# Chunks 0 and 1 as a pair: all eight units in the prologue, and chunk 1's second layer in a stretch of its own

## The chip, the cores and the metric

One NeuronCore of one Trainium2 chip runs the kernel. The metric is the device time of one execution in microseconds (us), lower is better. Engines are named as in the profile: PE (TensorE, the matmul array), PEld (its weight loads), DVE (VectorE), ACT (ScalarE), POOL (GpSimd), SP (the engine that here only issues DMAs); "ACTq" and "SPq" are the DMA-issuing sides of ACT and SP.

## The reference

Decayed linear attention over blocks of 64 tokens, and behind it a two-layer feed-forward network with softplus. 4 batches, 8 heads, 768 tokens, 64 dims a head; the network is 512 to 2048 to 512 over 3072 tokens. All of it is float32.

```python
for b in range(nb):                                   # blocks of 64 tokens, in order
    intra = (qb @ kb.T * Dmask) @ vb                  # Dmask[i,j] = lam**(i-j), lower triangle
    inter = (qb * lam_pow) @ kv_state
    out[:, :, sl] = intra + inter
    kv_state = lam**64 * kv_state + (kb * rev_pow).T @ vb
...
h = x @ w_in                                          # x: (3072, 512) from out
g = np.maximum(h, 0) + np.log1p(np.exp(-np.abs(h)))   # softplus
return g @ w_out
```

## The kernel before, in words

**Tiling.** The 768 tokens are six chunks of 128 tokens (two blocks of each of the 4 batches, so 512 rows for the network). The 8 heads are four pairs. A *unit* g is one chunk of one head pair: g = 4·chunk + pair, 24 units, each of two 512-KB loads (`load_upto`). A unit runs `q_decay` and `k_decay`, the scores and state products on PE (`mm_scores`, tiles x and y), `mask_scores`, the state update (`update_states`, which needs the state of the unit four earlier), then `mm_out` (tile z), which gives the network's input for that head pair. An `event(g)` is the output set of unit g−1 and the scores and update of unit g.

**The products of the network** are made of float32 values split in a high and a low part: three matmuls for each product. A weight matrix is 16 blocks f; block (f, 0) is of the first layer (A f in the change's lists) and (f, 1) of the second (B f). Each comes from DRAM as 64-bit words of 512 KB (`w_load`) and is converted on chip: `w_scale` and `w_round` on ACT, `w_shift`, `w_sign` and `w_add` on DVE, `w_hi` on ACT, `w_lo` on DVE; in the loop always for a pair of blocks at once, in the order of `w_order`.

**The chunks.** Chunks 0 and 1 use the plain network: `mlp1` is a first-layer block (12 matmuls of 128x512), `chain_act`, `chain_hi`, `chain_lo` make its softplus and the two parts, `mlp2` is the second-layer block (12 matmuls into four accumulators). Chunks 2 and 3, and 4 and 5, go as pairs whose first layer is done with seven products of half-size blocks (P1 to P7, L629), and the last pair's second layer too (L1014). These need sums of weight blocks (`block_sums`/`store_sums`/`send_sums`, or the same work as `box_sums`/`box_parts`/`box_send`), which are made on DVE and ACT during the earlier chunks, sent to DRAM (g1, g2 for the first layer, v for the second), and loaded back (`load_w1`); the converted blocks themselves go the same way (`store_blocks` to g1, g2, g3; `load_w2` brings second-layer blocks back).

**What sets the order.** Each engine works through its own instructions in the order in which the program writes them, and waits by semaphores. There is no planner: the prologue is a list of steps written out (L480 to L492, names resolved by the table at L472), the rest is loops. Before: the prologue has units 0 to 4 and first-layer blocks 0 to 3 of chunk 0. Then a loop over s = 4 to 31 (s // 16 is the chunk, s % 16 the block): the chain of block s−1, a conversion of the next weight pair, the second-layer block s−4, a unit now and then, and the first-layer block s; chunk 0 goes first, chunk 1 behind it. The sums for first-layer blocks 0 to 5 are made in chunk 1's part of that loop. In the first chunk the carry of the state from its first block to its second is made on PE: a matmul with zeros opens the accumulator (L306), and two matmuls with a diagonal matrix add the decayed state (L359); ACT copies the result (L364).

Of the kernel before, what the change touches and what calls it, by code (L numbers as in the profile page):

```python
# [7 lines left out]
F32 = mybir.dt.float32  # L8
# [7 lines left out]
C = 128  # L16
# [7 lines left out]
LAG = 4  # L24
STD = 2
# [7 lines left out]
def decay_attention_softplus_ffn(  # L33
# [119 lines left out]
    keep_warm(18)  # L153
# [22 lines left out]
    def powers(out, n):  # L176
# [125 lines left out]
    def mm_scores(g, x, y):  # L302
        q, k, kd, v = q_of(g), k_of(g), kds.pop(g), vt_of(g)
        if first_chunk(g):

            nc.tensor.matmul(y[lo], lhsT=warm[hi, :64], rhs=warm[hi], start=True, stop=False)  # L306
        for b in range(B):
            for t in range(2):
                cols = slice((2 * b + t) * 64, (2 * b + t + 1) * 64)
                for s in range(2):  # L310
                    r = half(s)
                    nc.tensor.matmul(x[r, cols], lhsT=k[r, b, t], rhs=q[r, b, t], start=True, stop=True)  # L312
                    if s == 0 or not last_chunk(g):
                        nc.tensor.matmul(
                            y[half(1 - s), cols], lhsT=kd[r, b, t], rhs=v[r, b, t],
                            start=s == 0 or not first_chunk(g), stop=s == 0 or not first_chunk(g),
                        )
# [37 lines left out]
    def carry_states(g, y):  # L355
        st = states[g]
        u = y[lo].rearrange("q (b t e) -> q b t e", b=B, t=2)
        for t in range(2):
            nc.tensor.matmul(  # L359
                u[:, :, t], lhsT=diag[hi, heads(g).start + t], rhs=st[hi, :, t], start=False, stop=t == 1  # L360
            )
# [37 lines left out]
    h_tiles, l_tiles, g_tiles, o_tiles = {}, {}, {}, {}  # L399

    def chain_act(s):
        l_tiles[s] = tl([128, 512], F32, f"l{s}")
        nc.scalar.activation(l_tiles[s], h_tiles.pop(s), AF.Softplus)  # L403

    def chain_hi(s):
        g_tiles[s] = t4([128, 2, 512], F32R, f"g{s}")
        nc.scalar.copy(out=g_tiles[s][:, 0, :], in_=l_tiles[s])  # L407

    def chain_lo(s):
        g = g_tiles[s]  # L410
        nc.vector.tensor_sub(out=g[:, 1, :], in0=l_tiles.pop(s), in1=g[:, 0, :])  # L411

    def mlp1(s, ps_=range(NP)):
        c, f = divmod(s, NF)
        if s not in h_tiles:
            h_tiles[s] = bank(f"h{s}")
        w = w_of(f, 0)
        for p in ps_:
            cs = slice(p * 128, (p + 1) * 128)
            x = x_of(c, p)  # L420
            for n, (i, j) in enumerate(((0, 0), (1, 0), (0, 1))):
                nc.tensor.matmul(  # L422
                    h_tiles[s], lhsT=w[:, i, cs], rhs=x[:, j, :],
                    start=p == 0 and n == 0, stop=p == NP - 1 and n == 2,
                )
# [661 lines left out]
```

## Time and profile before

Three runs took 584.24 to 584.87 us, median 584.67. The profiled execution took 585.31, of which the trace spans 583.4 from the first instruction to the last; its granted TensorE clock is 1.000.

| engine | busy us | share of the span | instructions |
|---|---|---|---|
| PE | 567.5 | 97% | 5155 |
| DVE | 394.3 | 68% | 612 |
| ACT | 277.7 | 48% | 446 |
| POOL | 4.1 | 1% | 11 |

The DMA queues moved 148.64 MB. In rows of the trace a name left of the arrow is what is written, right of it what is read; L and a number is the line of the kernel. Rows of groups end with the busy time, the mean of one instruction in ns, and the idle time of the engine just before them with what ended it. Matmuls overlap in the array, so the mean of one is longer than the distance from one start to the next.

### The profile page before, as it was taken

The numbers are of one execution on the slowest core, as the hardware profiler recorded it, in microseconds if no ns is written. First come the engines' busy times: TensorE is split into PE (matmuls) and PEld (weight loads), VectorE is DVE, ScalarE is ACT, GpSimd is POOL, SyncE is SP. The second block draws the span as 40 slices with busy tenths as digits, with TensorE's granted clock in tenths as the row PEclk, the third lists the DMA queues.
The fourth block names the chain that finished last, engine by engine and source line by source line (L and its number), as shares of the span: only waits on it lengthen the run. The fifth ranks groups of instructions, "written<-read, shape, count | busy, mean of one in ns | idle before, by whom it ended". The sixth has DMA issues, their size and how long they took to land.

```text
span 583.4 us, 12175 instructions
## 1 busy us (share of the span) xinstructions
PE 567.5 (97%) x5155; PEld 460.1 (79%) x5155; DVE 394.3 (68%) x612; ACT 277.7 (48%) x446; POOL 4.1 (1%) x11
## 2 busy tenths in 40 slices
PE   8999989999999999999999999999999999999997
PEld 6677767788888887887878888866888888788886
DVE  7779998975667867476655765459623646748983
ACT  3777776663445445444344433436323333454441
POOL 2000000000000000000000000000000000000000
PEclk9999999999999999999999999999999999999999
DMA  8997555899999678477774878699797336911701
GB/s 292 406 408 289 183 203 175 271 326 341 334 396 406 238 248 308 142 269 285 249 255 163 300 242 285 245 302 317 298 398 281 129 122 217 383 53 51 274 37 72
DMA packets 52534, 148.64 MB, mean 255 GB/s; under 512 B 4480, under 2 KB 20864, under 8 KB 46464
## 3 DMA queue, kind: packets, MB, share of 16 engines
q1 hardware_dynamic: 40384, 133.19, 63.1%
q10 hardware_dynamic: 12096, 14.68, 7.4%
q8 instruction: 40, 0.66, 0.4%
q14 instruction: 14, 0.11, 0.1%
HBM read 110.10 MB, written 37.75 MB: 253 GB/s over the span
## 4 chain that ended last, share of the span: by engine, by line
PE 74%; DVE 10%; DMA 9%; ACT 2%; ACTq 2%; issue 1%; SPq 1%; DVEq 0%
PE rP L1014 13%; PE o L648 13%; PE b L629 11%; PE h L422 10%; PE o L443 9%; PE c L629 7%; PE a L629 7%; DMA raw<-in_wts 5%; DMA g<-w 2%; PE x L312 2%; PE z L327 2%; DMA att<-in_att 2%; ACTq L573 2%; PE z L331 1%; DVE c L236 1%
## 5 line engine op out<-in xcount | busy, mean ns | idle before, releaser
L648 PE MATMUL o<-w,g 128*128 128x512 f32 x432 | 105.8, 394 | 2.0 <-DVE g L640 1.2
L422 PE MATMUL h<-x,w 128*128 128x512 f32 x384 | 94.7, 396 | 3.0 <-DVE w L243 2.1
L648 PEld LDWEIGHTS o<-w,g 128*128 128x128 f32 x432 | 79.9, 188 | 21.8 <-DVE g L640 3.3
L422 PEld LDWEIGHTS h<-x,w 128*128 128x128 f32 x384 | 70.9, 188 | 20.8 <-DVE w L243 3.7
L443 PE MATMUL o<-w,g 128*128 128x512 f32 x336 | 82.0, 393 | 1.1 <-DVE w L243 0.8
L1014 PE MATMUL rP<-sP,vP 128*128 128x512 f32 x336 | 76.3, 389 | 0.0
L443 PEld LDWEIGHTS o<-w,g 128*128 128x128 f32 x336 | 62.5, 188 | 15.0 <-DVE w L243 1.1
L1014 PEld LDWEIGHTS rP<-sP,vP 128*128 128x128 f32 x336 | 63.1, 188 | 13.1
L629 PE MATMUL b<-xcP,w1b 128*128 128x512 f32 x192 | 49.1, 391 | 1.3 <-DVE act L951 0.8
L629 PE MATMUL a<-xcP,w1a 128*128 128x512 f32 x192 | 48.8, 389 | 0.0
L403 ACT ACTIVATE l<-h 128x512 f32<-128x512 f32 x32 | 19.1, 598 | 58.9 <-PE h L422 56.3
L629 PEld LDWEIGHTS b<-xcP,w1b 128*128 128x128 f32 x192 | 35.8, 188 | 9.9 <-DVE ta L802 1.4
L629 PEld LDWEIGHTS a<-xcP,w1a 128*128 128x128 f32 x192 | 36.1, 188 | 7.5
L411 DVE TENSOR_TENSOR g<-l,g 128x512 fp32r<-128x512 f32 x32 | 22.0, 689 | 24.6 <-ACT g L407 24.5
L339 DVE TENSOR_TENSOR a<-x,mask 128x512 f32<-128x512 f32 x15 | 10.4, 691 | 38.6 <-PE x L312 20.3
L951 DVE TENSOR_TENSOR act<-b,ta 128x512 f32<-128x512 f32 x8 | 5.5, 691 | 31.1 <-PE b L629 31.1
L894 ACT CAST sP<-act 128x512 fp32r<-128x512 f32 x32 | 19.2, 619 | 13.0 <-PE rP L1014 6.8
L640 DVE TENSOR_TENSOR sP<-act,sP 128x512 fp32r<-128x512 f32 x32 | 20.9, 686 | 6.6 <-ACT sP L894 6.6
L629 PE MATMUL c<-xcP,w1b 128*128 128x512 f32 x96 | 24.4, 390 | 0.0
L629 PE MATMUL b<-xcP,w1a 128*128 128x512 f32 x96 | 24.4, 389 | 0.0
L629 PE MATMUL c<-xcP,w1a 128*128 128x512 f32 x96 | 24.4, 389 | 0.0
L387 ACT COPY xr<-z 128x512 f32<-128x512 f32 x16 | 9.4, 585 | 30.4 <-PE z L331 30.0
(133 smaller groups left out, 881.5 us busy)
## 6 DMA issues: line engine op xcount, KB each, us to landing
att<-in_att SPq DMA_DIRECT2D x48, 512.0 KB, 6.8
w<-g SPq DMA_DIRECT2D x23, 1024.0 KB, 7.9
raw<-in_wts SPq DMA_DIRECT2D x32, 512.0 KB, 10.2
w1a<-g SPq DMA_DIRECT2D x16, 1024.0 KB, 6.6
g<-w SPq DMA_DIRECT2D x24, 512.0 KB, 8.4
w1b<-g SPq DMA_DIRECT2D x16, 768.0 KB, 7.0
vP<-box ACTq DMA_DIRECT2D x32, 256.0 KB, 4.3
vP<-vP SPq DMA_DIRECT2D x8, 1024.0 KB, 8.4
```

The lines of the kernel that those rows point to most:

```text
L312: nc.tensor.matmul(x[r, cols], lhsT=k[r, b, t], rhs=q[r, b, t], start=True, stop=True)
L327: nc.tensor.matmul(w[half(t), s, cols], lhsT=st[r, b, t], rhs=qd[r, b, t], start=True, stop=False)
L403: nc.scalar.activation(l_tiles[s], h_tiles.pop(s), AF.Softplus)
L411: nc.vector.tensor_sub(out=g[:, 1, :], in0=l_tiles.pop(s), in1=g[:, 0, :])
L422: nc.tensor.matmul(h_tiles[s], lhsT=w[:, i, cs], rhs=x[:, j, :], start=p == 0 and n == 0, stop=p == NP - 1 and n == 2,)
L443: nc.tensor.matmul(o_tiles[c][b], lhsT=g[:, i, b * 128 : (b + 1) * 128], rhs=w[:, j], start=f == 0 and n == 0, stop=f == NF - 1 and n == 2,)
L573: nc.scalar.dma_start(out=v_sums[p][:, i], in_=parts[:, :, n])
L629: nc.tensor.matmul(to, lhsT=w[:, k, n, p * 128 : (p + 1) * 128], rhs=x[:, j, p], start=start and p == 0 and m == 0, stop=p == 1 and m == 2 ...
L640: nc.vector.tensor_sub(out=g[:, 1], in0=l, in1=g[:, 0])
L648: nc.tensor.matmul(outs[c, b], lhsT=g[:, i, b * 128 : (b + 1) * 128], rhs=w[:, j], start=f == 0 and n == 0, stop=f == NF - 1 and n == 2,)
L894: nc.scalar.copy(out=g[:, 0], in_=of)
L1014: nc.tensor.matmul(to, lhsT=w[:, k, x, n * 128 : n * 128 + 128], rhs=g[:, y], start=fresh and i == 0 and m == 0, stop=i == NF // 2 - 1 and ...
```

## The change

Chunks 0 and 1 are worked as a pair, and the state carry of the first chunk moves from PE to DVE.

- `w_order` begins with A0 to A3 and then takes two second-layer blocks B and two first-layer blocks A in turn. The first loads are A0, unit 0, A1, units 1 to 4, A2 and A3, units 5 and 6; the rest are issued inside the lists.
- The zero matmul, the diagonal matrix and its matmuls go; `carry_states`, `update_first` and `update_second` are pairs of DVE instructions.
- The prologue's list (not quoted whole: 16 lines of such steps as `m 1 2`, block 1 of chunk 0 with head pair 2) now holds all eight units of chunks 0 and 1, the first-layer blocks 0 to 6 of both chunks (`m`, `n`), second-layer blocks 0 to 3 of chunk 0 (`l2`), and the sums of box 0. The first warm-up has 24 matmuls in place of 18; further ones in the list are 8 in place of 13.
- The loop runs f = 7 to 15. Each turn has first-layer block f of chunk 0 and of chunk 1, a second-layer block of chunk 0 three or more blocks behind, a weight pair, and box sums. Chunk 1's softplus results wait in SBUF (`late_act`). Unit 8's scores and events 9 to 11 stand at f = 9, 11, 13, 15.
- Chunk 1's second layer follows in one stretch, with events 12 to 16 at f = 1, 4, 7, 10, 13, and with the inputs of chunks 2 and 3's products.
- All eight second-layer boxes are made in the loop of chunks 2 and 3; before, two of them were made in chunk 3's second-layer stretch, and boxes (0, 6) and (0, 7) in that loop. First-layer boxes are sent by ACT's queue (`box_send`); before, six of eight went by SP's.

The core of the diff:

```diff
-    w_order = [(f, 0) for f in range(LAG)]
-    for f in range(2):
-        w_order += [(f, 1), (f + LAG, 0)]
-    for f in range(2, NF, 2):
-        w_order += [(f, 1), (f + 1, 1)]
-        if f + LAG < NF:
-            w_order += [(f + LAG, 0), (f + LAG + 1, 0)]
+    w_order = [(f, 0) for f in range(4)]
+    for f in range(4, NF, 2):
+        w_order += [(f - 4, 1), (f - 3, 1), (f, 0), (f + 1, 0)]
+    w_order += [(f, 1) for f in range(NF - 4, NF)]
...
-    for n in range(NP - 1):
-        load_upto(n + 1)
-        w_load(n + 1)
-    load_upto(NP)
-    w_load(7)
-    load_upto(NP + 1)
+    w_load(1)
+    load_upto(1)
+    w_load(2)
+    load_upto(5)
+    w_load(4)
+    load_upto(7)
...
-        if first_chunk(g):
-
-            nc.tensor.matmul(y[lo], lhsT=warm[hi, :64], rhs=warm[hi], start=True, stop=False)
...
     def carry_states(g, y):
-        for t in range(2):
-            nc.tensor.matmul(
-                u[:, :, t], lhsT=diag[hi, heads(g).start + t], rhs=st[hi, :, t], start=False, stop=t == 1
-            )
-    def next_states(g, y):
-        nc.scalar.copy(out=states[g][lo].rearrange("q b t d -> q (b t d)"), in_=y[lo])
+        decayed(g, states[g][lo], states[g][hi], hi, y[lo].rearrange("q (b t e) -> q b t e", b=B, t=2))
+    def update_first(g, y):
+        decayed(g, states[g][hi], states[g][lo], lo, y[hi].rearrange("q (b t e) -> q b t e", b=B, t=2))
+    def update_second(g, y):
+        states[g + NP] = th([128, B, 2, D], F32, f"st_{g + NP}")
+        decayed(g, states[g + NP][lo], states[g][hi], hi, y[lo].rearrange("q (b t e) -> q b t e", b=B, t=2))
...
+    def late_act(f):
+        if f // 4 not in late_l:
+            late_l[f // 4] = t8([128, 4, 512], F32, f"lb1_{f // 4}")
+        nc.scalar.activation(late_l[f // 4][:, f % 4], h_tiles.pop((1, f))[0], AF.Softplus)
...
-    for s in range(LAG, last):
...
+    conv_at = {7: [(12, 13), (14, 15)], **{f: [(2 * f, 2 * f + 1)] for f in range(8, NF)}}
+    box_of = {8: 1, 9: 2, 10: 3, 11: 4, 12: 5, 14: 6}
+    event_of = {9: 2 * NP, 11: 2 * NP + 1, 13: 2 * NP + 2, 15: 2 * NP + 3}
+    n_l2 = 4
+    for f in range(7, NF):
+        unit = event_of.get(f)
+        if unit is not None:
+            k_decay(unit)
+            q_decay(unit)
+        for ks in converting:
+            w_hi(*ks)
+            w_lo(*ks)
+        mlp1(0, f)
+        converting = conv_at[f]
+        for ks in converting:
+            w_scale(*ks)
+            w_round(*ks)
+            w_shift(*ks)
+            w_sign(*ks)
+        chain_act(f)
+        chain_hi(f)
+        for ks in converting:
+            w_add(*ks)
+        chain_lo(f)
+        mlp1(1, f)
+        if boxed and f >= 8:
+            box_parts((0, boxed[0]))
+        if f in box_of:
+            box_sums((0, box_of[f]))
+        if n_l2 < f - 3:
+            second0(n_l2)
+            n_l2 += 1
+        late_act(f)
+        if unit is not None:
+            if unit == 2 * NP:
+                scores_of(unit)
+                keep_values(unit)
+            else:
+                event(unit)
+                second0(n_l2)
+                n_l2 += 1
+        if boxed and f >= 8:
+            box_send((0, boxed.pop(0)))
...
+    box_sums((0, 7))
+    store_second(7)
+    load_w2(0)
+    load_w2(1)
+    second0(NF - 3)
+    second0(NF - 2, NF - 1, ends=True)
+    box_parts((0, 7))
+    events = {3 * n + 1: 3 * NP + n for n in range(NP + 1)}
...
+    for f in range(NF - 2):
...
+        if f in extra:
+            extra[f]()
+        run(seconds(1, [(f, gs.pop(f), w2_tiles[f // 2][:, f % 2])]))
+        if f in events:
+            event(events[f])
...
-        box_at = [(0, NF // 2 - 2), (0, NF // 2 - 1)] + [(1, i) for i in range(2, NF // 2)]
+        box_at = [(1, i) for i in range(NF // 2)]
...
-            if f in (2, 4):
-                box_sums((1, f // 2 - 1))
```

Three places in the order of instructions. First ACT, from the end of turn f = 7 to f = 8 of the new loop, after the change. Names: l and g are chunk 0's softplus result and its high part, lb the late results of chunk 1, w the weight casts of `w_hi` (w_1204 is B4 and B5, w_1207 is A8 and A9), c and raw the conversion of the next pair.

```order
L384 ACTIVATE l_1175<-h_7_1152 128x512
L388 CAST g_1177<-l_1175 128x512
L398 ACTIVATE lb_1_995<-h_7_1182 128x512
L222 CAST w_1204<-c_1165 128x1024
L222 CAST w_1207<-c_1170 128x1024
L201 ACTIVATE c_1223<-raw_1196 128x1024
```

The same place on PE, after the change (h_7_1152 is chunk 0's block 7, h_7_1182 chunk 1's; o are the accumulators of the second layer):

```order
L409 MATMUL h_7_1182<-x_0_646,w_1001 128x512 x6
L409 MATMUL h_7_1182<-x_1_839,w_1001 128x512 x6
L409 MATMUL h_8_1210<-x_0_306,w_1207 128x512 x6
L409 MATMUL h_8_1210<-x_1_461,w_1207 128x512 x6
L409 MATMUL h_8_1234<-x_0_646,w_1207 128x512 x6
```

Block 8 of chunk 0 stands directly behind block 7 of chunk 1, whose softplus (lb_1_995) stands on ACT ahead of the casts of block 8's weights. Before the change each turn of the loop had one first-layer and one second-layer block, and ACT had no late results.

Second, DVE from the box sums of turn f = 9 to the conversion of f = 10, after the change (a is unit 8's masked scores, st its states, w_1400 the low part of A10 and A11):

```order
L513 TENSOR_TENSOR box_2_1326<-w_942 128x512 x2
L516 TENSOR_TENSOR box_2_1326<-box_2_1326 128x256
...
L319 TENSOR_TENSOR a_1379<-w_1346,mask 128x512
L324 SCALAR_TENSOR_TENSOR st_717<-st_717,lam_c,w_1346 64x4x64 x2
L324 SCALAR_TENSOR_TENSOR st_1383<-st_717,lam_c,w_1346 64x4x64 x2
L226 TENSOR_TENSOR w_1400<-c_1300,w_1400 128x1024
L209 TENSOR_SCALAR c_1416<-c_1416 128x1024
```

The low part of the weights of the next first-layer block stands behind the box sums and unit 8's mask and states.

Third, PE where chunk 1 ends and chunks 2 and 3 begin (a, b and c are the accumulators of the seven-product layer, xc its inputs). Before the change, behind the scores of event 16:

```order
L422 MATMUL h_2813<-x_0_758,w_1342 128x512 x6
L422 MATMUL h_2813<-x_1_1180,w_1342 128x512 x6
L648 MATMUL o_0_1808<-w_6_2532,g_2548 128x512 x3
...
L648 MATMUL o_3_1811<-w_6_2532,g_2677 128x512 x3
L629 MATMUL a_0_2880<-xcP_2170,w1a_2709 128x512 x6
L629 MATMUL b_0_2881<-xcP_2703,w1a_2709 128x512 x6
```

After the change, behind the same scores:

```order
L292 MATMUL x_2784<-att_2587 64x64
L294 MATMUL y_2785<-att_2587,kd_2710 64x64
L621 MATMUL a_0_2859<-xcP_2267,w1a_2590 128x512 x6
L621 MATMUL b_0_2860<-xcP_2692,w1a_2590 128x512 x6
L621 MATMUL c_0_2875<-xcP_2434,w1a_2590 128x512 x6
```

A first-layer block and two second-layer blocks of chunk 1 stood between the last scores and the first product; now nothing does.

More of the change, by code (lines that the diff above doesn't have):

```diff
@@ L452, in w_group, with second @@
-    def w_group(j):
-        return (2 * j, 2 * j + 1) if 2 * j < NW else ()
-    def scores_of(g):
-        w = work(f"w{g}")
-        mm_scores(g, w[:, 0], w[:, 1])
-        mask_scores(g, w[:, 0])
-        update_states(g, w[:, 1])
+                    to, lhsT=w[:, i, cs], rhs=x[:, j, :],
+                    start=not done and n == 0, stop=len(done) == NP - 1 and n == 2,
+                )
+            done.append(p)
+    n_second = {}
+    def second(c, f, b, g, w):
+        if (c, b) not in outs:
+            outs[c, b] = obank(f"o{c}_{b}")
+        k = n_second[c, b] = n_second.get((c, b), 0) + 1
+        for n, (i, j) in enumerate(((0, 0), (0, 1), (1, 0))):
+            nc.tensor.matmul(
+                outs[c, b], lhsT=g[:, i, b * 128 : (b + 1) * 128], rhs=w[:, j],
+                start=k == 1 and n == 0, stop=k == NF and n == 2,
+            )
@@ new lines, in finish, with seconds @@
+    def finish(c, b):
+        if c not in obs:
+            obs[c] = t8([128, B, 512], F32, f"ob{c}")
+        nc.scalar.copy(out=obs[c][:, b], in_=outs[c, b])
+        nc.scalar.dma_start(out=out[b * S + c * C : b * S + (c + 1) * C, :], in_=obs[c][:, b])
+    def seconds(c, fs, ends=False):
+        work_ = []
+        for f, g, w in fs if not ends else ():
+            work_ += [lambda f=f, g=g, w=w, b=b: second(c, f, b, g, w) for b in range(B)]
+        if ends:
+            for b in range(B):
+                for f, g, w in fs:
+                    work_.append(lambda f=f, g=g, w=w, b=b: second(c, f, b, g, w))
+                work_.append(lambda b=b: finish(c, b))
+        return work_
@@ L462, in decay_attention_softplus_ffn, with run, second0 @@
+    def run(work_, n=None):
+        for _ in range(len(work_) if n is None else min(n, len(work_))):
+            work_.pop(0)()
+    def second0(*fs, ends=False):
+        run(seconds(0, [(f, g_tiles.pop(f), w_of(f, 1)) for f in fs], ends))
     xy, z = {}, {}
@@ L576, in box_send @@
             nc.scalar.dma_start(out=g2[i][:, :, 1:3], in_=parts[:, :, 2:4])
-    def send_sums(i):
-        parts = ready.pop(i)
-        nc.sync.dma_start(out=g1[i][:, :, 2:4], in_=parts[:, :, 0:2])
-        nc.sync.dma_start(out=g2[i][:, :, 1:3], in_=parts[:, :, 2:4])
-    w1_tiles, w2_tiles = {}, {}
+    w1_tiles = {}
+    steps_of = {
+        "q": q_decay, "k": k_decay, "xy": begin, "a": lambda p: mask_scores(p, xy[p][0]),
+        "st": lambda p: first_states(p, xy[p][1]), "z": end, "dl": lambda p: carry_states(p, xy[p][1]),
+        "uh": lambda p: update_first(p, xy[p][1]), "ul": lambda p: update_second(p, xy[p][1]),
+        "xh": lambda p: x_high(p, z[p]), "xl": lambda p: x_low(p, z[p]),
+        "scale": w_scale, "round": w_round, "shift": w_shift, "sign": w_sign, "add": w_add, "hi": w_hi, "lo": w_lo,
+        "act": chain_act, "ghi": chain_hi, "glo": chain_lo, "bct": late_act, "l2": second0,
+        "m": lambda f, p: mlp1(0, f, (p,)), "n": lambda f, p: mlp1(1, f, (p,)),
+        "box": lambda i: box_sums((0, i)), "load": lambda *ks: w_load(ks[-1] + 1), "unit": load_upto, "warm": keep_warm,
+    }
@@ L585, in load_w1 @@
+    """.replace("\n", " ").split(","):
+        name, *words = line.split()
+        steps_of[name](*map(number, words))
     def load_w1(i):
@@ L862, in decay_attention_softplus_ffn @@
             if f + ahead < NF:
-                split(f + ahead)
+                split(c + 1, f + ahead)
             if f >= 1:
```

348 lines of the change are left out of this document (113 added, 235 removed).

## The prediction

> **What bounds the kernel now.** I read the page first, then the windows by stage, then the groups of the first stretch, and last the waits and the chain.
>
> From the page of before (busy time by engine; granted clock in 40 slices; DMA rate in 40 slices; the chain by engine; one row of the DMA issues):
>
> ```profile
> span 583.4 us, 12175 instructions
> PE 567.5 (97%) x5155; PEld 460.1 (79%) x5155; DVE 394.3 (68%) x612; ACT 277.7 (48%) x446; POOL 4.1 (1%) x11
> ...
> PEclk9999999999999999999999999999999999999999
> ...
> GB/s 292 406 408 289 183 203 175 271 326 341 334 396 406 238 248 308 142 269 285 249 255 163 300 242 285 245 302 317 298 398 281 129 122 217 383 53 51 274 37 72
> ...
> PE 74%; DVE 10%; DMA 9%; ACT 2%; ACTq 2%; issue 1%; SPq 1%; DVEq 0%
> ...
> w<-g SPq DMA_DIRECT2D x23, 1024.0 KB, 7.9
> ```
>
> TensorE is the bound, at full clock throughout. Only idle PE time, or PE time spent on nothing useful, can be won. The chain's 10% DVE and 9% DMA say that there is some; the windows say where (columns: stretch and length, then busy time and instruction count of PE, PEld, DVE, ACT, POOL, then clock, DMA share, GB/s):
>
> ```profile
> 0.00:60.30 60.30, 54.36 (x799) 40.65 (x799) 48.14 (x70) 40.15 (x64) 4.09 (x11) 1.00 0.92 350
> 60.30:93.00 32.70, 30.72 (x255) 24.26 (x248) 30.49 (x39) 22.99 (x31) 0.00 (x0) 1.00 0.53 177
> 93.00:229.00 136.00, 134.94 (x1772) 111.21 (x1771) 100.50 (x161) 69.36 (x110) 0.00 (x0) 1.00 0.87 308
> ```
>
> After 93 us PE is full (134.9 of 136.0). Before that it is DMA (share 0.92), then VectorE (30.5 of 32.7), that sets the pace. So the change can win only ahead of 93 us and can lose anywhere. What PE did in the first stretch (groups by form):
>
> ```profile
> L422 PE MATMUL h<-x,w 128*128 128x512 f32 x72 | 18.6, 403 | 0.0
> L151 PE MATMUL warm_ps<-warm 128*128 128x512 f32 x31 | 10.2, 478 | 1.4 <-DVE warm L146 1.4
> L443 PE MATMUL o<-w,g 128*128 128x512 f32 x36 | 9.0, 396 | 1.1 <-DVE w L243 0.8 <-ACT w L239 0.3
> L331 PE MATMUL z<-own,att 64*64 64x64 f32 x128 | 5.1, 231 | 1.9 <-issue 1.9
> L312 PE MATMUL x<-att 64*64 64x64 f32 x128 | 4.9, 222 | 0.0
> ...
> L359 PE MATMUL y<-st,spare 64*64 64x256 f32 x16 | 4.2, 379 | 0.0
> L312 PE MATMUL w<-att 64*64 64x64 f32 x64 | 2.3, 221 | 0.0
> L306 PE MATMUL y<-warm 64*64 64x512 f32 x4 | 1.8, 442 | 0.0
> ...
> L331 PE MATMUL z<-a,att 64*64 64x64 f32 x32 | 1.0, 218 | 0.0
> ```
>
> Means overlap, so I price by start to start, from the chain of waits (start, length, what):
>
> ```profile
> 4.59 9.82 DMA att<-in_att
> ...
> 123.47 2.72 PE o L443 x12
> 126.19 2.72 PE h L422 x12
> 128.91 2.72 PE o L443 x12
> 133.68 2.95 PE o L443 x12
> ```
>
> A group of 12 large matmuls is 2.72 us. Between 131.63 (128.91+2.72) and 133.68 lie one output set and one score set of a unit: 2.05 us, so a unit is taken at 2.1.
>
> **The change, part by part.**
>
> *1. The prologue.* By 60.3 us before has done 9 groups (72+36 matmuls), 6 score sets (128 and 64 at 32 a set) and 5 output sets (128 and 32): 24.5+11.6 = 36.1 us of useful work; 24.2 are lost. Useful work must reach what after has when its loop begins: 8 units (16.8), 14 first-layer groups (38.1) and 4 second-layer groups (10.9), 65.8 us. Before gets there 29.7 us of work later, plus the stalls in between. The waits of PE, 0 to 130 us (total, times, longest):
>
> ```profile
> PE h L422 <- DVE w L243: 2.1, 3, 1.3
> PE z L331 <- issue: 1.9, 2, 1.4
> ...
> PE y L314 <- DVE own L286: 0.9, 1, 0.9
> PE o L443 <- DVE w L243: 0.8, 1, 0.8
> ```
>
> With the refill of the array these stalls take 2.7 us: 92.7 us in all. After: the loads come in another order. At 406 GB/s a 512-KB block takes 1.29 us, and the chain's landing at 14.41 (4.59+9.82) is the eighth block. Counting on, with A0 now ahead of unit 0, the first scores move from 9.5 to about 10.1; unit 5's second block is number 16, at 27; unit 7's is 24, at 37.6; A6 and A7 are 27 and 28, at 42.7. Walking the list with these times and the durations below, PE waits for units and for A2 to A5 until about 47.5, with 29.1 us done, and then has work to the end, with 1.6 to 2 us of margin where it first meets the low parts of A4 to A7. The remaining 36.7 us end at 84.2. **Gain 8.5**; bounds 0 (two margins lost and further holes) and 12 (full from 44). The removed zero and diagonal matmuls (L306, 4; L359, 16) and L195 on VectorE lie inside this; the twelve state updates that replace them are 24 instructions on a VectorE that then carries about 67 of 84 us.
>
> Durations that I use, first VectorE, then ScalarE (groups by form: busy, mean ns):
>
> ```profile
> L344 DVE SCALAR_TENSOR_TENSOR st<-st,lam_c,y 64x256 f32<-64x256 f32 x52 | 22.9, 480 | 0.8
> L411 DVE TENSOR_TENSOR g<-l,g 128x512 fp32r<-128x512 f32 x32 | 22.0, 689 | 24.6 <-ACT g L407 24.5
> ...
> L236 DVE CUSTOM_DVE_ANT_0 c<-raw,c 128x2048 uint16<-128x2048 uint16 x13 | 15.9, 1226 | 1.7
> L230 DVE SCALAR_TENSOR_TENSOR c<-raw,c 128x1024 uint32<-128x1024 uint32 x13 | 15.9, 1225 | 0.5
> L243 DVE TENSOR_TENSOR w<-c,w 128x1024 fp32r<-128x1024 f32 x13 | 15.9, 1221 | 1.6 <-ACT w L239 1.6
> ...
> L566 DVE TENSOR_TENSOR box<-box 128x1024 fp32r<-128x1024 f32 x10 | 12.2, 1221 | 0.7 <-ACT box L565 0.7
> ...
> L339 DVE TENSOR_TENSOR a<-x,mask 128x512 f32<-128x512 f32 x15 | 10.4, 691 | 38.6 <-PE x L312 20.3 <-PE y L314 18.3
> ...
> L226 DVE TENSOR_SCALAR c<-c 128x1024 uint32<-128x1024 uint32 x13 | 8.9, 686 | 0.0
> ```
>
> ```profile
> L403 ACT ACTIVATE l<-h 128x512 f32<-128x512 f32 x32 | 19.1, 598 | 58.9 <-PE h L422 56.3 <-DVE g L411 2.5
> ...
> L239 ACT CAST w<-c 128x1024 fp32r<-128x1024 f32 x13 | 13.6, 1046 | 4.9 <-DVE c L236 4.9
> ```
>
> *2. The loop, f = 7 to 15.* The engines are in order, and this is where I expect the time to go back. At f=8, mlp1(0,8) needs the low part of A8 and A9. ScalarE takes late_act(7) first, which needs the end of mlp1(1,7); then come two weight casts, then VectorE's low part of the second pair. PE has nothing behind mlp1(1,7), since second0 runs only from f=8. Wait: 0.60 + 2×1.05 + 1.22 = 3.9, with hand-overs **4.0**.
>
> At f=10, mlp1(0,10) needs the low part of A10, and on VectorE it stands behind the sums of box 2 and unit 8's mask and four state updates. Unit 8's scores are the last that PE has. From them: mask 0.69, four updates 1.92, low part 1.22, 3.8 even if VectorE arrives free. It doesn't quite: its list since f=9's start (query decay, low parts, shift, sign, add, chain low, box parts, box sums, about 9.8 us) meets 9.3 of PE, so **4.6** with hand-overs. At f=12 and 14 a second0 of 2.72 stands behind the event and covers most: **1.1** and **0.9**. Sum **10.6**. Cross-check: the loop holds 89 us of VectorE work (ten conversions of 4.36, six box sums of 2.9, seven box parts, nine chain low parts, four units) against 81 us of PE (18+9 groups, 7 half units), so some 8 are due unless VectorE enters far ahead. Before's own stall there (0.44, at 113.9) goes. Bounds: 7.8 (the two floors) and 14.
>
> *3. Behind the loop.* On SP's queue load_w2(0) stands behind store_second(7), which waits for the low part of the last pair (B14, B15); a load lands 7.9 us after its issue (page). From that low part PE has 5.44 us in second0(14, 15) and some of second0(13), and then chunk 1's second layer needs the tile: **+1.5** (0 to 3).
>
> *4. End of chunk 1's stretch.* Event 16 now stands directly ahead of P1. Before, mlp1(31) and two second-layer groups lay between. P6's second part needs mask, states, three differences and a cast behind event 16: some 2.7 us of wait against the 0.9 here (waits of PE, 130 us to the end):
>
> ```profile
> PE o L648 <- DVE g L640: 1.2, 2, 0.9
> PE h L422 <- DVE a L339: 0.9, 1, 0.9
> PE o L648 <- ACT g L636: 0.9, 1, 0.9
> ```
>
> So **+1.8** (0 to 3).
>
> *5. Chunk 3's stretch.* Boxes (1,0) and (1,1) leave it, and with them the two waits for g L640: **−1.2** (0 to −2.5). The third row, at 385, is ScalarE issuing four box DMAs; they stay.
>
> *6. Queues.* The first-layer boxes leave on ScalarE's queue inside the loop, two DMAs a turn, ahead of the next weight cast; stores and raw blocks run there too. **+1** (0 to 4): ScalarE is about 70% loaded there, by my sum, so most of it hides.
>
> Sum: −8.5 + 10.6 − 0.4 + 1.5 + 1.8 − 1.2 + 1 = **+4.8**. The profiled execution took 585.31 (span 583.4 plus 1.9 around it), 0.64 above the median of 584.67. On the median: 589.5.
>
> A page's rule on such waits: the Trainium skill, "TensorE: Matmul & The Clock Gate", section "Part 1: The HAM clock gate", says that PE falls to half its clock after an idle window of about 3.4 us and needs as long, busy, to come back. In before the longest wait of PE behind its start is 1.4 us at clock 1.00, so no row here shows it for or against.
>
> **The rivals.**
>
> *A. The clock drops in the waits (593.5).* Both long waits of part 2 (4.0 and 4.6) exceed any that before has. If the clock halves behind each, the next work loses about 2 us twice, as the first warming matmuls do, which come at half pace: 589.5 + 4. For it: the lengths. Against: a wait must fill a whole window, which one of 4 us may straddle.
>
> *B. Faster, by the prologue (581).* One mechanism: PE is already full at 43 to 44 us, because the units of chunk 1 give it work while A2 to A7 land, and each hole before that is filled. Then the gain is 12, the loop costs its floor of 7.8, and the queues nothing: −12 + 7.8 − 0.4 + 0.5 + 1.5 − 1.2 = −3.8, 580.9. It decides for faster where the gain passes the loop's cost by 2; at the floor that is from about 9.5. For it: 24.2 us are lost before 60 us in before. Against: the blocks land no sooner than 1.29 us apart, and each pair's conversion takes 4.36 of VectorE.
>
> *C. A wash (584.7).* Gain 10.5, loop 8.6, parts 3 to 6 together 2.3.
>
> *D. DMA as the loop's bound (596).* Raw blocks, stores and boxes, about 34 MB in 95 us, near the 308 GB/s that the third window averages; a raw pair that lands 2 us late in three of the turns adds 6.
>
> **How the numbers follow.** The forecast (586.5 to 592.5) 0.50, A 0.13, B 0.18, C 0.12, D 0.07. About 0.2% (1.2 us) is what a measurement can tell from no change. Faster 0.18 (B), same 0.12 (C), slower 0.70. The range of 8 in 10 takes in C, the forecast, A, the upper third of B and D's near half: 581.5 to 597.
>
> **What would show it.** Right: no PE idle time between about 48 and 84 us; mlp1(0,8) waiting some 4 us for the weight's low part, with late_act(7) and two casts just ahead of it on ScalarE; mlp1(0,10) waiting over 3.8 us, released by the low part behind four state updates; shorter waits at f=12 and 14; a wait of 2 to 3 us between event 16 and chunk 2's first products; chunk 3's stretch without its two waits. Wrong: PE waits in the loop below 7 us in sum, a prologue that ends before 81 us or after 88, or a granted clock under 1.00 behind the long waits.

## The result, and the profile after

The changed kernel takes 603.12 us (median of four runs, 599.41 to 604.65) against 584.61 before: ratio 1.0308, 95% interval 1.026 to 1.0356. It is slower, as forecast, but by 18.5 us and not by 4.8, which is outside the range of 581.5 to 597. The profiled execution took 604.65, 19.3 more than that of before.

The page of the changed kernel (rows as for before; the last is the queue that brings PE its own program):

```profile
span 602.8 us, 12127 instructions
PE 574.5 (95%) x5136; PEld 468.0 (78%) x5136; DVE 393.6 (65%) x609; ACT 274.6 (46%) x438; POOL 3.9 (1%) x10
...
PEclk9889999879999899999999999999999999999999
...
q8 instruction: 40, 0.66, 0.4%
```

PE has 19 matmuls fewer and is busy 7 us longer: matmuls at half clock last longer (those of 128x512 start 0.43 us apart there, and 0.23 us apart at full clock). The windows of the changed kernel by stage (columns as before, clock ahead of the DMA share):

```profile
0.00:60.00 60.00, 50.98 (x1058) 39.87 (x1059) 42.43 (x68) 30.72 (x49) 3.93 (x10) 0.91 0.80 302
60.00:93.00 33.00, 33.00 (x147) 27.35 (x146) 25.95 (x34) 18.75 (x25) 0.00 (x0) 1.00 0.41 138
93.00:120.00 27.00, 23.49 (x90) 18.65 (x89) 16.78 (x21) 14.64 (x19) 0.00 (x0) 0.87 0.28 89
120.00:150.00 30.00, 26.20 (x282) 21.02 (x281) 25.80 (x40) 14.77 (x21) 0.00 (x0) 0.89 0.90 315
...
190.00:235.00 45.00, 42.03 (x536) 34.29 (x531) 24.94 (x44) 18.46 (x34) 0.00 (x0) 0.96 0.99 386
```

From 60 to 93 us PE is full at full clock, as forecast. Four stages run below full clock, where before has none. When does the loop begin? Its first block is the 24 matmuls of 128x512 of turn 7 in the timeline of PE:

```profile
94.16 5.60 PE L409 MATMUL h<-x,w 128*128 128x512 f32 x24
102.33 0.50 PE L409 MATMUL h<-x,w 128*128 128x512 f32 x1 [2.56 <-ACT w L222]
103.78 1.65 PE L409 MATMUL h<-x,w 128*128 128x512 f32 x3 [0.95 <-DVE w L226]
```

At 94.2, where the forecast had 84.2 and before does the same work by 92.7. So ten of the missing 14 us are lost ahead of the loop. What PE waits for there (timeline of PE, the rows with a wait for "issue", which is time without anything that the profile shows as awaited):

```profile
19.34 0.21 PE L292 MATMUL x<-att 64*64 64x64 f32 x1 [2.32 <-issue]
...
25.59 0.37 PE L292 MATMUL x<-att 64*64 64x64 f32 x1 [2.88 <-issue]
...
31.69 0.21 PE L292 MATMUL x<-att 64*64 64x64 f32 x1 [0.28 <-issue]
...
37.84 0.27 PE L294 MATMUL y<-att,kd 64*64 64x64 f32 x1 [1.75 <-issue]
```

From start to start these four cost 7.9 us. The clock of 0.91 up to 60 us comes on top: 0.09 of 60 us is 5.4 us at most, part of which fell into the stalls themselves. The scores that stall are those of units 2 to 5, whose second loads had landed at 15.7, 19.3, 21.8 and 27.0. Counting matmuls and their weight loads in the trace gives what they have in common, in both kernels, beside the DMA records of queue 8 (16 KB each):

```
kernel   PE instructions before the stall   block on queue 8 lands   PE goes on
before   442, 696, 950                      16.4, 22.5, 28.8         17.7, 23.8, 30.3
after    440, 694, 948, 1204                17.9, 24.1, 30.4, 36.5   19.3, 25.6, 31.7, 37.8
```

The stalls come at the same counts, 254 or 256 apart, and end 1.3 to 1.5 us after a block of 256 instructions has landed; the blocks come every 6.2 us. PE waits for its own program. Its stall rows stand in the waits of before too ("issue", 1.9 and 0.6 us), and the forecast read past them. The Trainium skill, "Runtime: NRT & Kernel Launch", section "Instruction fetch mechanics", says that an engine fetches its program in blocks of 16 KB, 256 instructions, and that crossing one is mostly hidden. The first agrees; the second does not here.

The loop and what follows (waits of PE, 93 to 260 us):

```profile
PE h L409 <- DVE w L226: 5.6, 4, 3.2
PE h L409 <- ACT w L222: 3.4, 3, 2.6
PE o L422 <- DMA w<-g: 3.0, 1, 3.0
PE b L621 <- ACT xcP L593: 0.9, 1, 0.9
PE a L621 <- DVE a L319: 0.8, 1, 0.8
```

These are the waits of the forecast, at their places. At f = 8 the order on ScalarE is the one read from the program (timeline of ACT): `late_act`, then both casts; the next scale stands behind them:

```profile
99.80 0.60 ACT L398 ACTIVATE lb<-h 128x512 f32<-128x512 f32 x1 [1.47 <-PE h L409]
100.29 1.98 ACT L222 CAST w<-c 128x1024 fp32r<-128x1024 f32 x2
```

And at f = 10 the low part follows mask and states (timeline of DVE), PE going on at 128.35:

```profile
124.55 0.68 DVE L319 TENSOR_TENSOR a<-w,mask 128x512 f32<-128x512 f32 x1
125.25 1.79 DVE L324 SCALAR_TENSOR_TENSOR st<-st,lam_c,w 64x256 f32<-64x256 f32 x4
127.07 1.23 DVE L226 TENSOR_TENSOR w<-c,w 128x1024 fp32r<-128x1024 f32 x1
```

Behind each long wait the clock falls (windows of 2 us around f = 8; the number ahead of the DMA share is the clock):

```profile
100.00:102.00 2.00, 0.00 (x0) 0.00 (x0) 0.64 (x1) 2.00 (x3) 0.00 (x0) 1.00 0.00 0
102.00:104.00 2.00, 0.72 (x2) 0.41 (x3) 2.00 (x3) 2.00 (x3) 0.00 (x0) 0.72 0.00 0
104.00:106.00 2.00, 2.00 (x5) 1.62 (x6) 1.83 (x3) 0.36 (x1) 0.00 (x0) 0.50 0.00 0
106.00:108.00 2.00, 2.00 (x6) 1.55 (x5) 0.95 (x1) 0.00 (x0) 0.00 (x0) 0.50 0.05 6
```

Half clock lasts until about 109: some 3.2 us of work lost here, and by the same reading 2.6 behind f = 10 and 1.7 behind the wait for w<-g at 204.

### The profile page after: what moved, and what is told of

It is laid out like the page before. It is cut to its first block, busy times and chain, and to the rows that moved or that the text cites. A ratio compares the mean times of both kernels' runs of the same rounds, so it can differ in the third digit from the quotient of the medians.

```text
span 602.8 us, 12127 instructions
## 1 busy us (share of the span) xinstructions
PE 574.5 (95%) x5136; PEld 468.0 (78%) x5136; DVE 393.6 (65%) x609; ACT 274.6 (46%) x438; POOL 3.9 (1%) x10
## 3 DMA queue, kind: packets, MB, share of 16 engines
q10 hardware_dynamic: 15936, 22.02, 10.2%
## 4 chain that ended last, share of the span: by engine, by line
PE 80%; DMA 9%; DVE 6%; issue 2%; ACT 1%; SPq 1%; ACTq 0%; DVEq 0%
PE o L422 25%; PE rP L974 13%; PE h L409 12%; PE b L621 10%; PE c L621 7%; PE a L621 6%; DMA raw<-in_wts 3%; PE x L292 3%; PE z L307 2%; DMA g<-box 2%; PE z L311 2%; DMA att<-in_att 2%; DMA w<-g 1%; DMA g<-w 1%; DVE st L324 1%
## 5 line engine op out<-in xcount | busy, mean ns | idle before, releaser
L422 PE MATMUL o<-w,g 128*128 128x512 f32 x768 | 184.9, 394 | 3.0 <-DMA w<-g 3.0
L422 PEld LDWEIGHTS o<-w,g 128*128 128x128 f32 x768 | 144.1, 189 | 34.1 <-ACT g L628 3.4
L409 PE MATMUL h<-x,w 128*128 128x512 f32 x384 | 100.4, 417 | 9.0 <-DVE w L226 5.6
L409 PEld LDWEIGHTS h<-x,w 128*128 128x128 f32 x384 | 76.1, 202 | 27.9 <-DVE w L226 6.9
L319 DVE TENSOR_TENSOR a<-x,mask 128x512 f32<-128x512 f32 x19 | 13.1, 691 | 49.2 <-PE y L294 29.5
L292 PE MATMUL x<-att 64*64 64x64 f32 x736 | 29.7, 226 | 5.5 <-issue 5.5
L324 DVE SCALAR_TENSOR_TENSOR st<-st,lam_c,y 64x256 f32<-64x256 f32 x76 | 33.4, 479 | 1.2
L292 PEld LDWEIGHTS x<-att 64*64 64x64 f32 x736 | 26.3, 139 | 8.7 <-issue 7.7
L632 DVE TENSOR_TENSOR g<-lb,g 128x512 fp32r<-128x512 f32 x32 | 21.8, 687 | 11.2 <-ACT g L628 11.0
L294 PE MATMUL y<-att,kd 64*64 64x64 f32 x544 | 22.8, 224 | 2.2 <-issue 1.8
```

Of the source, the lines that this page charges most:

```text
L294: nc.tensor.matmul(y[half(1 - s), cols], lhsT=kd[r, b, t], rhs=v[r, b, t], start=True, stop=True,)
L319: nc.vector.tensor_mul(out=a, in0=x.rearrange("q (b t i) -> q b t i", b=B, t=2), in1=m)
L324: nc.vector.scalar_tensor_tensor(out=to[:, :, t], in0=of[:, :, t], scalar=lam_c[r, h : h + 1], in1=u[:, :, t], op0=ALU.mult, op1=ALU.add,)
L409: nc.tensor.matmul(to, lhsT=w[:, i, cs], rhs=x[:, j, :], start=not done and n == 0, stop=len(done) == NP - 1 and n == 2,)
L422: nc.tensor.matmul(outs[c, b], lhsT=g[:, i, b * 128 : (b + 1) * 128], rhs=w[:, j], start=k == 1 and n == 0, stop=k == NF and n == 2,)
L632: nc.vector.tensor_sub(out=g[:, 1], in0=l, in1=g[:, 0])
```

## The experiments

Diffs are against the changed kernel unless another is named.

**x1_fill: the half clock behind the loop's waits.**

```diff
+        if f in (8, 10):
+            h_tiles[0, f] = bank(f"h0_{f}"), []
+            fill(h_tiles[0, f][0], 17)
         mlp1(0, f)
...
     box_parts((0, 7))
+    outs[1, 0] = obank("o1_0")
+    fill(outs[1, 0], 13)
```

> Extra matmuls into the accumulators that are opened next fill three long waits of PE: 17 ahead of mlp1(0,8), 17 ahead of mlp1(0,10), 13 ahead of chunk 1's first second-layer block (0.227 us each, so 3.9, 3.9 and 3.0 us). Nothing is done sooner. Theory 'the waits drop the clock': the granted clock stays 1.00 from 93 to 235 us; by the changed kernel's windows the half clock behind the three waits costs 3.2, 2.6 and 1.7 us, so 603.1 - 7.5 = 595.6. Rival 'the clock falls for another reason' (the load on the chip, or the prologue's half clock going on): the same slices stay at 0.5 and the time at 603.

598.28 us (597.1 to 602.6; ratio to before 1.0248, 1.02 to 1.0297). The windows of this run:

```profile
93.00:120.00 27.00, 27.00 (x119) 22.07 (x118) 19.03 (x24) 15.69 (x21) 0.00 (x0) 1.00 0.31 104
120.00:150.00 30.00, 28.56 (x301) 22.89 (x300) 27.85 (x44) 16.59 (x21) 0.00 (x0) 1.00 0.95 341
```

Full clock, with 47 useless matmuls more and the median 4.8 us lower (the ranges of the two kernels' runs overlap, 597.1 to 602.6 and 599.4 to 604.7; the windows are the firmer sign). From turn 7 to the end it is 503.0 us against 508.6, so 5.6 of the 7.5 expected. The waits do drop the clock. The prologue keeps its own (0.89 up to 60 us).

**x6_more_instr: what the prologue's stalls hang on.**

```diff
-    keep_warm(24)
+    for _ in range(96):
+        nc.tensor.matmul(warm_ps[:, :128], lhsT=warm[:, :128], rhs=warm[:, :128], start=True, stop=True)
```

> The first warm-up is 96 matmuls of 128x128 in place of 24 of 128x512: the same PE time, 144 instructions of PE more ahead of the first scores; loads and all else stay. Theory 'PE waits for its own instructions, in blocks of 256': the four stalls put down to issue, which now begin behind instructions 440, 694, 948 and 1204 (matmuls and weight loads counted) and end at 19.3, 25.6, 31.7 and 37.8 us, come at the same counts, so about 3 us earlier: they end near 16, 22, 28 and 35. Rival 'PE waits for the units' loads': they end at the same times as now. Time about the same, 603 (602 to 606).

609.64 us. The 96 narrow matmuls took 20.7 us, not 8.5, so the times of the expectation are void and the first scores began at 22.1. The counts are not: PE stalls before instructions 696, 950 and 1204 again, now in other work (timeline of PE in this run):

```profile
33.07 0.39 PE L312 MATMUL z<-own,att 64*64 64x64 f32 x10 [1.89 <-issue]
...
39.26 0.39 PE L312 MATMUL z<-own,att 64*64 64x64 f32 x10 [1.38 <-issue]
...
44.94 0.27 PE L308 MATMUL z<-own,st 64*64 64x64 f32 x2 [1.33 <-issue]
```

These are output sets of units 1 to 3, whose masked scores were done by 29.6, 32.2 and 38.3 us, before the stalls began. The loads don't set the stalls; the count does.

**x12_burst: what the blocks wait for.** (A first form of it, x10_burst, wrote 300 matmuls to one place; they followed each other at 0.117 us, too slow to run out of instructions, and it told nothing: 638.38 us.) Both expectations count half of the instructions: the trace has two matmul records, each with a weight load, for every matmul of the program, so x10 has 1200 PE instructions more and x12 has 768.

```diff
+    def burst(n):
+        to, other = obank("bx"), obank("by")
+        for _ in range(n):
+            ...
+                        nc.tensor.matmul(to[r, cols], lhsT=k_of(5)[r, b, t], rhs=q_of(5)[r, b, t], start=True, stop=True)
+                        nc.tensor.matmul(
+                            other[half(1 - s), cols], lhsT=k_of(5)[r, b, t], rhs=q_of(5)[r, b, t], start=True, stop=True
+                        )
...
-        uh 5, xy 6, m 3 2,
+        uh 5, xy 6, burst 6, m 3 2,
```

> The changed kernel with 300 extra 64x64 matmuls (600 PE instructions) ahead of m 3 2, at about 47.5 us, where the DMA engines are nearly idle (share 0.00 to 0.16 from 46 to 54 us); their results are overwritten. Theory 'the blocks come late because data transfers fill the DMA engines': the fetches then follow each other faster than every 6.2 us, 4 us or less, and the stalls between are under 1 us. Rival 'the fetch has a fixed round trip': 6.2 us between fetches here too, with stalls of 2 us or more at every 256 instructions. Time: 603 plus about 10.

> The changed kernel with six extra score sets' worth of 64x64 matmuls (192 of them, 384 PE instructions, laid out as the scores are, results unused) ahead of m 3 2 at about 47.5 us, where the DMA engines are nearly idle. Theory 'the blocks come late because data transfers fill the DMA engines': fetches follow each other within 4 us, stalls under 1 us. Rival 'the fetch has a fixed round trip': 6.2 us between fetches, with stalls of 2 us or more at multiples of 256 instructions. Time: 603 plus 4 to 10.

610.89 us, one run. The timeline of PE in the burst, and the windows of that time:

```profile
51.48 0.27 PE L548 MATMUL bx<-att 64*64 64x64 f32 x1 [1.36 <-issue]
...
54.93 0.27 PE L548 MATMUL bx<-att 64*64 64x64 f32 x1 [1.36 <-issue]
```

```profile
50.00:56.00 6.00, 3.28 (x177) 2.93 (x170) 0.00 (x0) 0.00 (x0) 0.00 (x0) 1.00 0.01 3
```

The stalls are there with idle DMA engines too (share 0.01), at counts 1970 and 2226, but 3.45 us apart; the blocks of queue 8 start every 3.4 to 3.8 us, against 6.0 to 6.3 earlier in the same run, while loads fill the DMA engines. Both theories were half right: with the DMA engines idle the blocks still come no faster than one in about 3.5 us, and with them full one comes in about 6.2. It is one run; the changed kernel's own blocks come faster too where the loads pause (3.7 us apart from 47 to 55 us, without a stall).

**x15_wide: the prologue with fewer instructions.**

```diff
+        if g < 2 * NP:
+            for b in range(B):
+                cols = slice(2 * b * 64, (2 * b + 2) * 64)
+                for s in range(2):
+                    r = half(s)
+                    nc.tensor.matmul(x[r, cols], lhsT=k[r, b, 0], rhs=q[r, b], start=True, stop=True)
+                    nc.tensor.matmul(y[half(1 - s), cols], lhsT=kd[r, b, 0], rhs=v[r, b], start=True, stop=True)
+            return
```

> The changed kernel with the score and state products of units 0 to 7 made for both heads of a pair by one matmul of twice the width (the second head's scores and states are then those of the first head's k, so that part of the result is left out): 32 matmuls a unit in place of 64, the same columns streamed, 512 PE instructions fewer in the prologue; loads, VectorE and ScalarE as before. Theory 'the prologue is paced by blocks of 256 PE instructions, and the half clock comes from those stalls': the stalls put down to issue (7.9 us in sum) fall under 3, the clock up to 60 us stays over 0.97, and the first block of turn 7 begins at 87 in place of 94 us: 603.1 - 7 = 596. Rival 'the prologue is paced by the loads and VectorE': it begins at 93 or later: 602.

591.98 us (590.36 to 594.19; ratio 1.0137, 1.0112 to 1.0162): 11.1 less than the changed kernel, where 7 were expected. The windows, the waits up to 93 us and the timeline at turn 7, of this run:

```profile
0.00:60.00 60.00, 56.72 (x847) 43.55 (x848) 51.89 (x79) 38.63 (x59) 3.91 (x10) 1.00 0.88 330
```

```profile
PE z L315 <- issue: 0.2, 1, 0.2
```

```profile
83.83 5.60 PE L417 MATMUL h<-x,w 128*128 128x512 f32 x24
```

With loads, VectorE and ScalarE as they were, the stalls are gone, the clock is 1.00, and turn 7 begins at 83.8, where the forecast had put it (84.2). The 32 wide matmuls of a unit take PE about 1.0 us, as the 64 narrow ones do, so the gain is not in the array's own time. This settles the prologue.

**x9_late_less** takes instructions out in a small way, on top of x8_late_first (below):

```diff
-    keep_warm(24)
+    keep_warm(8)
...
-        xy 0, warm 4,
+        xy 0,
...
-        xy 1, warm 4,
+        xy 1,
```

> The same, and 16 of the first 24 warming matmuls and the two later groups of 4 taken out: 48 PE instructions fewer ahead of the units. Theory 'the prologue is paced by blocks of 256 PE instructions': the stalls stay at the same instruction counts and end at about the same times, but with 48 instructions more of useful work done: 48/256 of 6.2 us, so 1.2 us less than the run without this edit. Rival 'warming counts for more than instructions': a colder start, half clock in the first scores, the same time or 1 to 2 us more.

594.55 us, 2.4 under x8's 596.94, although the clock up to 60 us is 0.83 against 0.91 there. In the profiled executions turn 7 begins at 91.2 against 92.4, the 1.2 us that were expected: fewer instructions were worth more than the warmth. The rest stands elsewhere: from 190 to 235 us the clock is 1.00 here and 0.92 in x8, and that this edit made the difference is not shown.

**x3_load: the queue ahead of chunk 1's second layer.**

```diff
-    store_second(7)
     load_w2(0)
     load_w2(1)
+    store_second(7)
```

> load_w2(0) and load_w2(1) stand ahead of store_second(7) on SP's queue, so they no longer wait for the last pair's low part. Theory 'queue order': the wait of 3.1 us ahead of chunk 1's second layer goes, and with it 1.7 us of half clock: 603.1 - 4.8 = 598.3. Rival 'the load is late because the DMA engines are full' (share 0.99 there): it lands at the same time, 603.

597.88 us (597.53 to 598.32; ratio 1.023, 1.0214 to 1.0245), near the 598.3 expected, and no wait for w<-g is left. That wait was queue order, not bandwidth. The size is less sure than the agreement looks: in the profiled execution turn 7 begins at 92.5 against 94.2, which the edit does not touch, and the clock in the loop is 0.94 against 0.87 and 0.89, while the waits there are 2.5 us longer.

**x2_same_turn and x8_late_first: mending the loop's order.**

```diff
-        for ks in converting:
-            w_hi(*ks)
-            w_lo(*ks)
         mlp1(0, f)
...
             w_add(*ks)
+        for ks in converting:
+            w_hi(*ks)
         chain_lo(f)
+        for ks in converting:
+            w_lo(*ks)
```

> Each weight pair's cast and low part are done in the turn that scales it, ahead of late_act, box sums, mask and state updates, in place of the start of the next turn. Theory 'the order on ScalarE and VectorE makes the loop's waits': the waits at f = 8, 10, 12 and 14 (4.0, 4.1, 0.8 and 1.0 us) fall to 2 us in sum, and the half clock behind the first two (5.8 us) goes with them: 603.1 - 8 - 5.8 = 589.3. Rival 'VectorE is simply full there' (89 us of work against 81 on PE): waits of 6 us in sum remain, in other places and shorter, the clock stays up: 593.

597.43 us. The waits for w are nearly gone, but (waits of PE, 93 to 260 us):

```profile
PE y L294 <- ACT lb L398: 8.2, 3, 4.0
PE h L409 <- DVE w L226: 0.9, 1, 0.9
```

The cast now waits on ScalarE for VectorE's w_add, and late_act behind it holds the bank that the next event's y needs. x8 puts late_act first, and adds x3's edit and event 16 at f = 12:

```diff
+        late_act(f)
+        if f > 7:
+            for ks in converting:
+                w_hi(*ks)
+                w_lo(*ks)
...
-    events = {3 * n + 1: 3 * NP + n for n in range(NP + 1)}
+    events = {(1, 4, 7, 10, 12)[n]: 3 * NP + n for n in range(NP + 1)}
```

> Three edits on the changed kernel: (1) each pair's cast and low part in its own turn as before, but late_act stands ahead of the cast (at f = 7 both pairs are done ahead of chain_act), (2) load_w2(0) and (1) ahead of store_second(7), (3) event 16 one turn earlier, at f = 12, so that a second-layer block stands between it and P1. Theory 'the order makes the waits; a waiting instruction holds up late_act, which frees the bank of the next event's y': the waits of 3.8 and 4.1 us for lb at the events are gone, waits of PE from 93 to 260 us sum to under 3 us, the clock stays 1.00 behind 60 us: 597.9 (the run with the load alone) - 8.5 (loop waits) - 4.5 (half clock in the loop) - 2.4 (event 16) = 582.5. Rival 'VectorE is full in the loop': 4 us or more of waits return somewhere in the loop: 586.5 or more.

596.94 us, against 582.5 expected, and x3's edit alone had 597.88: the new order and event 16 add 0.9 us, and the ranges of the two overlap. Its waits (93 to 260 us):

```profile
PE o L422 <- ACT ob L430: 2.8, 2, 1.5
PE h L409 <- DVE a L319: 2.8, 2, 2.0
PE x L292 <- ACT l L384: 2.5, 2, 1.4
PE y L294 <- ACT lb L398: 2.0, 3, 0.8
```

Ten us again, each for something else. Four runs ask what sets this.

**x11_early, x16_raw_ahead, x13_send, x14_only_send.** x11, x16 and x13 are made on x9, x14 on the changed kernel. x11 converts two pairs in the prologue's tail and each later pair a turn earlier; x16 only loads the raw blocks a turn earlier; x13 and x14 send the first-layer boxes and chunk 0's outputs by SP:

```diff
-    conv_at = {7: [(12, 13), (14, 15)], **{f: [(2 * f, 2 * f + 1)] for f in range(8, NF)}}
+    conv_at = {f: [(2 * f + 2, 2 * f + 3)] if f < NF - 1 else [] for f in range(7, NF)}
...
-            w_load(2 * f + 4)
+            w_load(2 * f + 6)
...
-            nc.scalar.dma_start(out=g1[i][:, :, 2:4], in_=parts[:, :, 0:2])
+            nc.sync.dma_start(out=g1[i][:, :, 2:4], in_=parts[:, :, 0:2])
...
+        eng = nc.scalar if c else nc.sync
+        eng.dma_start(out=out[b * S + c * C : b * S + (c + 1) * C, :], in_=obs[c][:, b])
```

> On top of the run with the three edits and less warming: the pairs A8/A9 and B4/B5 are converted in the prologue's tail, where VectorE and ScalarE stand idle behind the chain of block 7 (VectorE busy 6 to 7 of the 13 us ahead of 93), each later pair a turn earlier, and the raw blocks are loaded a turn earlier. Theory 'VectorE is idle before the loop and full in it (18.5 of 20 us from 110 to 130)': 8.7 us of its work leave the loop, the waits from 110 to 190 (9 us in sum) fall to 3, and the half clock behind them goes: 594.6 - 6 - 2 = 586.5. Rival 'the waits come from the round trips between ScalarE and VectorE, not from the amount': they stay at 7 or more: 593.

> The run with the three edits and less warming, with each turn's raw blocks loaded one turn earlier (B6 and B7 in the prologue's tail). Theory 'the raw blocks land on the edge of the turn that needs them' (ScalarE's scale waits 4 to 7 us in sum for them in the loop): those waits go, and PE's waits from 110 to 190 fall from 9 to 5: 594.6 - 5 = 589.6. Rival 'VectorE and the banks' release set the pace': 593 to 596.

> On top of the run with the three edits and less warming (594.6): the first-layer boxes and chunk 0's outputs are sent by SP's queue in place of ScalarE's. Theory 'ScalarE's own DMA issues hold up its in-order queue' (each pair of sends waits there for VectorE's low part, then takes 1.1 to 1.8 us to issue; behind it stand kd, the next scale and the softplus that frees the bank of the next event): PE's waits for ScalarE's l, lb and ob (9 us in sum from 130 to 200) fall to 3, with the half clock behind them: 594.6 - 6 - 2 = 586.5. Rival 'VectorE's amount of work sets the pace': the same waits under other names: 593 or more.

> The changed kernel with this edit alone. The prediction's term 6 put the sends at 1 us (0 to 4): 602.1, and not under 599. If the sends decide when the loop's long waits end, f = 8 and f = 10 wait under 3 us each and the time is 597 or less.

All four missed: x11 602.52, x16 597.51, x13 632.60, x14 630.74 us. In x14 SP waits at each send for VectorE's low part, and the raw blocks and w2 loads behind it come late (waits of PE, whole run):

```profile
PE o L422 <- DMA w<-g: 9.4, 1, 9.4
PE h L409 <- DVE w L226: 7.0, 3, 5.7
```

The DMA engines are busy for 0.74 of the time from 93 to 235 us, so this is order, not bandwidth. SP's queue has no room for such a wait; the sends' place on ScalarE's is the better one. In x16 ScalarE still waits for VectorE (waits of ACT, 93 to 190 us):

```profile
ACT w L222 <- DVE c L219: 11.4, 6, 3.3
ACT kd L273 <- DVE box L517: 7.0, 2, 3.5
```

x11 made a wait of 3.1 us of its own ahead of the loop (turn 7 began at 97.8) and still had 9 us in it. So neither less work for VectorE in the loop nor earlier raw blocks helped. A chain of in-order queues remains: VectorE works on box sums, ScalarE waits for it with softplus and casts behind, PE waits for the bank. That it is this chain is read from the waits, not shown by a run that removes it.

**x17_best: what helped, together.**

```diff
-        bct 5, l2 1, box 0, glo 6
+        bct 5, box 0, glo 6
...
+            fill(h_tiles[0, f][0], 5 if f == 8 else 16)
...
+        if f == 7:
+            second0(1)
```

(with the edits of x3, of event 16 and of x9)

> What helped, put together on the changed kernel: load_w2 ahead of store_second(7), event 16 one turn earlier, less warming, second-layer block 1 moved from the prologue's tail behind mlp1(1,7), and extra matmuls (5 and 16) that fill the rest of the waits at f = 8 and f = 10 and keep the clock up. Sum by the single runs: 597.9 (load alone) - 2.4 (event) - 2.4 (warming) - 2.7 (block 1 in the wait) - 5.3 (half clock behind f = 8 and f = 10) = 585.1, about the time of the kernel before. Rival 'the waits come back elsewhere, as in the runs with mended order': 591 or more.

590.40 us (589.36 to 592.03; ratio 1.0109, 1.0089 to 1.0128). It is 12.7 under the changed kernel, the best whole version, and still 5.7 behind the kernel before. Its windows show where it got:

```profile
93.00:120.00 27.00, 27.00 (x177) 21.60 (x175) 22.98 (x33) 17.67 (x22) 0.00 (x0) 1.00 0.55 187
120.00:150.00 30.00, 28.21 (x242) 22.98 (x242) 26.51 (x37) 16.24 (x22) 0.00 (x0) 1.00 0.94 344
```

The loop is at full clock and nearly full; 21 of its matmuls (4.8 us) are filling. It fell 5.3 short of the sum: the terms overlap (x3's run, the base of the sum, had a higher clock in the loop than the changed kernel's profile, 0.94 against 0.87 and 0.89).

## Why the prediction was right or wrong

By its own parts, in us, forecast against measured (profiled executions):

| part | forecast | measured | from |
|---|---|---|---|
| 1 prologue | -8.5 | +1.5 | turn 7 at 94.2, before at 92.7 |
| 2 loop's waits | +10.2 | +9.5 | 4.0, 4.1, 0.8, 1.0 start to start, less 0.4 of before |
| 3 load_w2 | +1.5 | +3.1 | wait for w<-g |
| 4 event 16 | +1.8 | +1.5 | 2.5 against 1.0 |
| 5 chunk 3's stretch | -1.2 | -2.5 | no wait of PE left from 399 to 423 |
| 6 queues | +1 | not separated | |
| half clock in the loop and at the load | 0 (rival A: 4) | +7.5 | windows; x1 gave back 5.6 |

The measured parts sum to 20.6; the difference of the executions is 19.3. Part 1's figure has the half clock of the prologue in it.

**Part 1 failed**, at "Walking the list with these times and the durations below, PE waits for units and for A2 to A5 until about 47.5, with 29.1 us done". The walk had loads and engines in it and not PE's own program. A unit is 224 PE instructions in chunk 0 and 256 in chunk 1 for 2.1 us of work, a group of the network 24 for 2.7. By 47.5 us the walk needs some 2090 of them (1920 for the units, 108 for four and a half groups, 64 for warming); 440 by 17.9 us and 256 every 6.2 us from there give some 1660, an estimate from the rows above. x15 needs 512 fewer, some 1580, and has no such stall; it shows that the rest of the walk held: 83.8 against 84.2, and 592.0 us in all, 2.5 above the forecast. The rows that would have told were in the view that part 1 quotes ("issue": 1.9 of waits in before, with five units); the forecast gave them no term, and they grow with the units. One step of the walk does not add up as written: the block that lands at 14.41 is the seventh of 512 KB and not the eighth, and eight blocks of 1.29 from there give 24.7 and not 27. The times themselves were right (27.0, 37.3 and 42.4 us measured, against 27, 37.6 and 42.7).

**Parts 2 and 4 were right** in mechanism and nearly in size: reading the order of two in-order engines and adding durations gave 4.0 and 4.6 for waits that measured 4.0 and 4.1. **Part 5** had the right sign: its two waits went, but so did the third, which the forecast kept, and that one is 1.0 of the 2.5. **Part 3** was right in mechanism (x3) and half in size.

**The second step that failed is the half clock, which the sum put at nothing.** Rival A was true at once with the forecast, and should have been no rival: the waits that the forecast itself put at 4.0 and 4.6 us were the condition for it. The reason given against it, that a wait must fill a whole window, did not hold: at f = 8 PE waited 2.6 us and then 1.0, neither of them the 3.4 us that the prediction names, and half clock followed. Its price was too low (3.2 and 2.6 us, not 2 each), and it also came behind the stalls of the prologue and the wait for w<-g. **Rival D** (the loop bound by DMA) did not happen: from 93 to 190 us the kernel moved 281 GB/s, and none of the loop's long waits is for a DMA. (Its 34 MB in 95 us would be 358 GB/s, above the 308 that it calls near.) **Rival B's** early prologue did not come; x15, where the instructions came in time, gains 8.9 us of its 12.

## What to carry to other kernels

Count instructions as well as time: many small matmuls close together, while loads fill the DMA engines, can run PE out of program, and the sign is a wait for "issue" that recurs about every 256 instructions. A forecast that adds a wait of several us on PE must add the half clock behind it, here 1.7 to 3.2 us more. Where engines are in order and wait for each other, mending one wait mostly moved it here: x2 and x8, which reordered, got 6 us where 14 and 21 were expected, and in x8 5 of them come with x3's edit. x17, which left the order and put work and filling into the waits, is 4.2 us under x9, which has the mended order and the same three other edits.

## What the runs showed of the hardware that was not expected

PE's program came in blocks of 256 instructions every 6.2 us with full DMA engines and every 3.5 us with idle ones, and PE went on about 1.4 us after a block landed.

The clock did not need a wait of its full window. The Trainium skill ("TensorE: Matmul & The Clock Gate", section "Part 1: The HAM clock gate") names an idle window of about 3.4 us, free-running; here half clock came in or just behind waits of 2.9 and 3.0 us, and one of 1.75 us at 37.8 (clock 0.51 from 38 to 40), and not behind one of 2.3 us at 19.3 (1.00 from 18 to 24). With the same stalls the clock up to 60 us was 0.91 in the changed kernel's profile, 0.89 in x1's and 0.97 in x3's. The changed kernel's runs spread over 5 us, those of before over 0.6; that the clock makes this spread fits (the mean clock is 0.982 in the shortest and 0.976 in the two longest), but no run here tests it.

The 96 narrow warming matmuls of x6 kept PE busy from 1.45 to 22.2 us and did not bring up its clock: the scores behind them still start at half pace (four in 0.11 us, against 0.055 in the changed kernel), where 24 wide ones have full pace from 7.3 us.
